# Where the additions of z run, where fourteen early gelus stand, five more warm-up matmuls and another order of banks in a linear-attention and GEGLU kernel

## The chip, the cores and the metric

The kernel runs on one core of a Trainium2 chip. A core has a matmul engine (TensorE, PE in the profile; its weight loads are shown as PEld), three engines for elementwise work (VectorE or DVE, ScalarE or ACT, GpSimd or POOL), and SyncE (SP), which here issues nearly all DMAs. Matmuls write PSUM, a memory of eight banks; everything else lives in SBUF, and inputs and output lie in HBM. The metric is the device time of one execution in microseconds (us); lower is better.

## The reference

One input x of 2048 tokens by 576 channels is normalised (xn) and goes through two branches, whose outputs are added to x. Branch A is linear attention with 32 heads of 18 channels. Branch B is a GEGLU feed-forward network with 4608 hidden channels.

```python
xn = layernorm(x)
# A: linear attention
q, k, v = split_heads(xn @ wqkv)                       # 32 heads of 18 channels
phi = lambda t: where(t > 0, t + 1, exp(t)) + 1e-6
pq, pk = phi(q), phi(k)
kv  = einsum("bhsd,bhse->bhde", pk, v)
z   = einsum("bhsd->bhd", pk)                          # sum of phi(k) over all tokens
o   = (pq @ kv) / (pq . z + 1e-6)
# B: feed-forward
ffn = (gelu(xn @ w_gate) * (xn @ w_up)) @ w_down
out = x + merge_heads(o) @ wo + ffn
```

The change deals with z, the sum of phi(k) over the 2048 tokens, and with the first hidden units of branch B.

## The kernel before

Tokens lie in 16 tiles of 128 (n = 0 to 15). The 4608 hidden channels are 36 units of 128, and the feed-forward part runs in four rounds of 512 tokens.

**First stage.** A tile of x is loaded, normalised on VectorE or ScalarE, and transposed into xnT: tiles 0 to 3 with TensorE (L337), the others with DMA transposes (L345). Then TensorE computes K for all 16 tiles and Q for the first four, and between them the gate and up projections of the first 14 hidden units (RAW = 14) for the first 512 tokens, whose raw results are copied out as they are (`_Raw`, copy L444). The list `line` gives PE's order: k0, q0, k1, q1, k2, k3, g0 to g3, K4, g4, K5, g5 and so on to K13, g13, K14, K15, Q2, Q3. A small letter is a token computed with whole 128-row matmuls (L408); a capital K or Q and every g is done in two parts, p1 and p2 (L245), in which two 64-row halves of the array write two banks and then swap. An empty instruction on GpSimd (the "turn", L256) stands between the two parts. The p1 of a unit comes one unit ahead of the p2 of the unit before it.

After p2 of a K, ScalarE computes exp (L420), VectorE clamps it (L423, "clamp") and adds the positive part of K from PSUM (L429, "phi"); the result is pk. Only then is the unit's pair of banks free. Five early tokens (RAW_T: k0, q0, k1, q1, k3) are first copied raw (L415), and their exp, clamp and phi are done later, from about 40 us on. Each unit takes two banks from a ring of eight (`banks`, L119), so a K takes over the pair of the K two tokens earlier, and a g that of the g two units earlier. The head tokens (k0 to k3, q0, q1) use a ring of their own over banks 4, 5, 6, 7, 2, 3; the transposes use banks 0 and 1, and the warm-up matmuls (`spin`, L226: 35 products of a zero tile) bank 7.

The order of this stage is made by a small planner: every piece of work is a `step` with an engine, a length, a rank and what it comes after. `in_order` (L66) plays the steps through with these lengths and emits, on each engine, the able step of the lowest rank number next; a step with a high number is emitted only where nothing else can run. On the chip each engine then runs its own list strictly in this order.

**Additions of z.** pk of tiles 4 to 13 are added into z_sum on GpSimd (L548, nine instructions, the first of which adds tiles 4 and 5), each held back until the turn of K two tokens later; pk of tiles 0 to 3 are added into z_dve on VectorE (L550); tiles 14 and 15 follow in the Gram stage, where z_sum and z_dve are added into z_bf (L632). In all this is nine instructions on GpSimd and six on VectorE.

**Gram.** G = xnᵀ pk is computed in five products (`gram` L563, `gram_last` L571), each over all 16 token tiles into two banks, and copied to g_sb, one half by ScalarE and the other by VectorE (`gram_copy`, L579). Then `kv_part` multiplies G with the V weights, `z_stage` sums z_bf over the partitions with a matmul by ones, and `mask_pair` keeps the heads' own blocks. Between these, `gelu_now` (L558) finishes the 14 raw units: gelu of the raw gate on ScalarE (L560), times the raw up on VectorE (L561). Eleven of them stand between the products, three behind the mask. The four bank pairs of Gram come up again in the feed-forward part after the ring has been stepped three pairs further (L651).

**Feed-forward.** `gu_pair` (L730) does two hidden units: p1, p1, p2, p2, then per unit the gelu (L753) and the product with up (L754). After 36 units `_DownTile` (L829) multiplies with w_down and adds the attention part and x. The weights of the last twelve w_down rows (wd_c) are loaded over the memory of the raw up results.

Of the kernel before, what the change touches and what calls it, by code (L numbers as in the profile page):

```python
# [9 lines left out]
ALU = mybir.AluOpType  # L10
# [4 lines left out]
P = 128  # L15
# [70 lines left out]
def kernel(  # L86
# [29 lines left out]

    SYNC = mybir.DependencyInfo(mybir.DependencyClass.Sync, mybir.DependencyReason.DATA)
    LO, HI = slice(0, HP), slice(HP, P)
    banks, head_banks = _Ring(list(range(8))), _Ring([4, 5, 6, 7, 2, 3])  # L119

    def two_banks(ring=banks):
        return [ring.next(), ring.next()]
# [28 lines left out]
    xn = apool.tile([P, NS, XW], BF16, name="xn")  # L151
    g_sb = apool.tile([P, KT, D], BF16, name="g_sb")
    z_sum = apool.tile([P, D], F32, name="z_sum")
    z_dve = apool.tile([P, D], F32, name="z_dve")
    z_bf = apool.tile([P, D], BF16, name="z_bf")

    def load_x(n0, cnt, on=nc.sync):
# [130 lines left out]
    def step(name, engine, took, rank, after, call, ready=0.0, tail=0.0):  # L288
        steps[name] = _Step(engine, took, rank, after, call, ready, tail)
# [68 lines left out]
        load(("x", n), 0.58, 295, 7.0 + 2.5 * (n - 10), [], lambda n=n: load_x(n, 2), ready=6.0)  # L358

    for n in range(NS):  # L360
        first = 1.5 * n if n < 4 else 11.0 + 3.0 * (n - 4)
        both = n // 2 * 2
        after_x = [("x", both)] if n >= 4 else []
        x_at = X_AT[n] if n < 4 else 0.0
        if n < 4:
            step(("twin", n), "POOL", 0.2, first, [], lambda n=n: x_twin(n, 1), ready=x_at)
        elif n == both:
            step(("twin", n), "POOL", 0.25, first, after_x, lambda n=n: x_twin(n, 2))
        twin = ("twin", n if n < 4 else both)
        for h in range(2):  # L370
            step(("stats", n, h), "DVE", 0.42, first, after_x, lambda n=n, h=h: ln_half(n, h), ready=x_at)
        step(("aggr", n), "DVE", 0.16, first, [("stats", n, 0), ("stats", n, 1)], lambda n=n: ln_aggr(n), tail=0.05)
        if n < 6:
            step(("rstd", n), "ACT", 0.46, first, [("aggr", n)], lambda n=n: ln_rstd(n, 1))
        elif n == both:
            step(("rstd", n), "ACT", 0.46, first, [("aggr", n), ("aggr", n + 1)], lambda n=n: ln_rstd(n, 2))
        ready = [("rstd", n if n < 6 else both), twin]
        if NORM[n] == "A":
            step(("bias", n), "POOL", 0.27, first, ready[:1], lambda n=n: ln_bias(n))
            ready.append(("bias", n))  # L380
        on, took = ("ACT", 0.92) if NORM[n] == "A" else ("DVE", 0.45)
        if n < HEAD:
            for i, (k0, k1) in enumerate(((0, TP_CUT), (TP_CUT, KT))):
                c0, c1 = k0 * P, k1 * P
                step(("norm", n, i), on, took * (c1 - c0) / XW + 0.05, first, ready, lambda n=n, c0=c0, c1=c1: ln_norm(n, c0, c1), tail=0.05)
                step(("tp", n, i), "PE", 0.06 * (k1 - k0), 0, [("norm", n, i)] + ([("xnT", n - 1, i)] if n else []), lambda n=n, i=i: transposes(n, i), tail=0.15)
                eng = "DVE" if i else "ACT"
                step(("xnT", n, i), eng, 0.26 if i else 0.48, first, [("tp", n, i)], lambda n=n, i=i: tp_copy(n, i), tail=0.02)
            steps[("xnT", n)] = _Step("none", 0.0, first, [("xnT", n, 0), ("xnT", n, 1)], lambda: None, 0.0, 0.0)
        else:  # L390
            step(("norm", n), on, took, first, ready, lambda n=n: ln_norm(n), tail=0.05)
            load(("xnT", n), 1.25, 80, first + 2, [("norm", n)], lambda n=n: dma_transposes(n))
# [97 lines left out]
    for name in line:  # L490
        kind, n = name[0], int(name[1:])
        if kind == "t":
            for i in range(2):
                pe(("tp", n, i), 0, [], None)
            continue
        u = _Chain()
        u.name, u.at = name, clock
        if kind in "kq":
            t = _Token(kind.upper(), n, head_banks)
            for h in range(2):  # L500
                free = owner.get(tuple(t.banks), [])
                pe((kind, n, h), 0.6125, [("xnT", n)] + free, lambda t=t, h=h: t.whole(h), ready=W_AT[kind.upper()])
                if kind == "k" and h == 0 and n + 1 < HEAD:
                    for i in range(2):
                        pe(("tp", n + 1, i), 0, [], None)
            later = name in RAW_T
            if later:
                step(("raw", name), "ACT", 0.72, clock, [(kind, n, 1)], t.raw)
            ready, rank = (LATER, 60.0) if later else (0.0, clock)
            step(("exp", name), "ACT", 0.72, rank, [("raw", name) if later else (kind, n, 1)], t.exp, ready=ready)  # L510
            step(("clamp", name), "DVE", 0.25, rank, [("exp", name)], t.clamp)
            step(("phi", name), "DVE", 0.76, rank, [("clamp", name)], t.phi, tail=0.05)
            owner[tuple(t.banks)] = [("raw" if later else "phi", name)]
            clock += 1.35
            continue
        if kind in "KQ":
            u.body = _Token(kind, n)
            b = u.body.banks
            after = [("xnT", n), ("w", "twin")]
            t1, u.t2 = 0.615, 0.49  # L520
            u.p1 = u.body.unit.rows
            u.swap = u.body.unit.swap
            u.unit_p2 = u.body.unit.p2
            at = 0.0
        else:
            u.body = _Raw(n)
            b = u.body.two
            blk = n // GUB
            after = [("xnT", m) for m in range(TPC)] + ([("gu", blk, i) for i in range(2)] if blk else [])
            t1, u.t2 = 1.08, 0.865  # L530
            u.p1 = u.body.rows
            u.swap = lambda body=u.body: body.unit.swap()
            u.unit_p2 = lambda body=u.body: body.unit.p2()
            at = 0.0 if blk else 9.1
        after += owner.get(tuple(b), [])
        pe(("p1", name), t1, after, u.p1, ready=at)
        step(("turn", name), "POOL", 0.06, clock, [("p1", name)], u.swap, tail=0.05)
        clock += t1 + u.t2
        pending.append(u)
        if len(pending) == 2:  # L540
            p2_step(pending.pop(0))
    while pending:
        p2_step(pending.pop(0))

    def z_add(on, dst, n, first):
        on.tensor_tensor(out=dst[:], in0=pk[:, n - 1, :] if first else dst[:], in1=pk[:, n, :], op=ALU.add)

    for n in range(HEAD + 1, NS - 2):  # L548
        step(("z", n), "POOL", 1.30, 6.0, [("turn", f"K{n + 2}"), ("phi", f"K{n}")], lambda n=n: z_add(nc.gpsimd, z_sum, n, n == HEAD + 1))
    for n in range(1, HEAD):  # L550
        step(("z", n), "DVE", 0.80, 52.0, [("phi", f"k{n - 1}"), ("phi", f"k{n}")] + ([("z", n - 1)] if n > 1 else []), lambda n=n: z_add(nc.vector, z_dve, n, n == 1))

    for name in in_order(steps):
        steps[name].call()
# [69 lines left out]
    on_banks = [two_banks() for _ in range(4)]  # L624
    gelus = list(range(RAW))
    gram(0, on_banks[0])
    gelu_now(gelus.pop(0))
    for n in range(NS - 2, NS):
        z_add(nc.vector, z_dve, n, False)
    gram_copy(0, on_banks[0])  # L630
    gram(1, on_banks[1])
    nc.vector.tensor_tensor(out=z_bf[:], in0=z_sum[:], in1=z_dve[:], op=ALU.add)  # L632
    for _ in range(2):
        gelu_now(gelus.pop(0))
    gram_copy(1, on_banks[1])
    gram(2, on_banks[2])
    for _ in range(4):
        gelu_now(gelus.pop(0))
    gram_copy(2, on_banks[2])
    gram_last(on_banks[3])  # L640
    gelu_now(gelus.pop(0))
    gram_copy(4, on_banks[3])
    gram(3, on_banks[0])
    for _ in range(3):
        gelu_now(gelus.pop(0))
    gram_copy(3, on_banks[0])
    b4, b1 = on_banks[1]
# [3 lines left out]
    for _ in range(3):  # L651
        two_banks()
    mask_pair(kvT, b4, b1)
    for f in gelus:
        gelu_now(f)

    asmall_cm.__exit__(None, None, None)
    awork_cm.__exit__(None, None, None)
# [71 lines left out]
    def gu_pair(sc, k):  # L730
        blk = sc * NB + k
        units = []
        aside = m_last_unit() if blk == M_UNIT else None
        if aside:
            aside.p1()
        for i in range(GUB):
            b = two_banks()
            u = gu_unit(blk, i, b, nc.gpsimd)
            if blk > RAW // GUB:
                load_gu(blk + NWBUF - 1, i)  # L740
            u.p1()
            units.append((b, u))
        if sc == 0 and k == RAW // GUB:
            load_wo()
        elif wd_left:
            load_wd(*wd_left.pop(0))
        if aside:
            aside.p2()
            m_last_copy(aside)
        for i, (b, u) in enumerate(units):  # L750
            u.p2()
            gl = fwork.tile([P, SC], F32, name="gl")
            nc.scalar.activation(out=gl[:], in_=ps_all[:, b[0], :], func=ACT.Gelu_apprx_tanh)  # L753
            nc.vector.tensor_tensor(out=hT[:, GUB * k + i, :], in0=ps_all[:, b[1], :], in1=gl[:], op=ALU.mult)  # L754
            if den_jobs and ((i == 1 and 0 < k < NB - 1) if sc else 8 < k < 17):
                job, n = den_jobs.pop(0)
                job(n)
# [186 lines left out]
```

## Time and profile before

The median of three runs is 515.73 us (515.57 to 515.77).

| what | value |
|---|---|
| profiled execution, its own time | 515.68 us |
| its span, first to last instruction | 513.9 us |
| PE busy | 505.3 us, 98% |
| VectorE busy | 229.9 us, 45% |
| ScalarE busy | 152.9 us, 30% |
| GpSimd busy | 20.7 us, 4% |
| first K matmul (L408) | at 6.66 us |
| K4, the first K done in two parts | at 24.57 us |
| Gram begins (L566) | at 64.40 us |
| first unit of the feed-forward loop (L245 behind L593) | at 84.00 us |

How to read it: a group's line gives source line, engine, operation, what is written and read, shapes, then how often, busy time, the mean of one in nanoseconds, and the idle time of the engine just before, with what ended it. A line of the order of time begins with start and length in us; "idle before" stands in brackets with its releaser. A line of the waits gives who waited for whom, the total in us, how many times, and the longest. Busy times of engines overlap, so they do not add up to the span. Matmuls overlap in the array and their ends are modelled, so the distance from start to start tells their rate better than the length of one.

### The profile page before, as it was taken

The page shows a single profiled execution, that of the slowest core. Times are in us where ns is not written, and L with a number is a line of the kernel's source. Part 1 is how long each engine was busy: PE and PEld are TensorE (multiplying, and loading weights), DVE is VectorE, ACT ScalarE, POOL GpSimd, SP SyncE. Part 2 cuts the span into 40 slices and gives each one's busy share as a digit, 9 for nine tenths or more (in the row PEclk, how much of TensorE's full clock was granted, in tenths as well). Part 3 has the DMA queues.
Part 4 walks back from the last instruction along what each step waited for, and adds up shares of the span by engine and source line. Part 5 has one row for each costly group of instructions (what it writes and reads, how often), then busy time and mean ns, then how long its engine had stood idle before and what let it go on. Part 6 is the DMA issues. An engine that isn't in the chain of part 4 may idle for free.

```text
span 513.9 us, 11032 instructions
## 1 busy us (share of the span) xinstructions
PE 505.3 (98%) x4686; PEld 309.2 (60%) x4686; DVE 229.9 (45%) x473; ACT 152.9 (30%) x265; POOL 20.7 (4%) x41
## 2 busy tenths in 40 slices
PE   8999899999999999999999999999999999999997
PEld 6587576444877544444777544445777544445774
DVE  6937886567000665555000765554101655544101
ACT  4878454333200432233000523323000533222000
POOL 2114400000000000000000000000000000000000
PEclk9999999999999999999999999999999999999999
DMA  9989902996210345665000356564000465740000
GB/s 262 258 172 237 282 2 66 280 255 165 63 63 1 117 144 163 177 163 147 13 11 1 116 164 173 152 168 136 13 13 4 134 174 147 163 131 14 13 13 23
DMA packets 113610, 61.56 MB, mean 120 GB/s; under 512 B 23250, under 2 KB 113562, under 8 KB 113562
## 3 DMA queue, kind: packets, MB, share of 16 engines
q1 hardware_dynamic: 113418, 60.72, 45.1%
q8 instruction: 36, 0.59, 0.5%
q10 hardware_dynamic: 144, 0.15, 0.1%
q14 instruction: 12, 0.10, 0.1%
HBM read 53.75 MB, written 2.36 MB: 109 GB/s over the span
## 4 chain that ended last, share of the span: by engine, by line
PE 93%; DVE 4%; DMA 1%; issue 0%; POOL 0%; ACT 0%; SPq 0%; DVEq 0%; POOLq 0%
PE ps_all L245 57%; PE ps_all L859 28%; PE ps_all L566 3%; PE ps_all L864 3%; PE ps_all L408 1%; DVE hT L429 1%; DVE stats L296 1%; DVE phi_e L423 1%; DMA wqkv_sb<-in_A_wqkv_dram 1%; DMA x_sb<-in_A_x_dram 1%; PE ps_all L847 0%; PE ps_all L574 0%; PE ps_all L337 0%; PE ps_all L593 0%; DVE pq L429 0%
## 5 line engine op out<-in xcount | busy, mean ns | idle before, releaser
L245 PE MATMUL ps_all<-xnT,wg 64*128 64x512 bf16 x1152 | 273.5, 376 | 0.0
L245 PE MATMUL ps_all<-xnT,wu 64*128 64x512 bf16 x1152 | 273.4, 376 | 0.0
L245 PEld LDWEIGHTS <-wg 64*128 64x128 bf16 x1152 | 108.3, 94 | 65.2
L245 PEld LDWEIGHTS <-wu 64*128 64x128 bf16 x1152 | 108.3, 94 | 64.5
L754 DVE TENSOR_TENSOR hT<-ps_all,gl 128x512 bf16<-128x512 f32 x130 | 89.9, 692 | 105.7 <-ACT gl L753 105.6
L859 PEld LDWEIGHTS <-hT 128*128 128x128 bf16 x1152 | 110.9, 98 | 30.9 <-issue 1.3
L753 ACT ACTIVATE gl<-ps_all 128x512 f32<-128x512 f32 x130 | 77.6, 597 | 165.4 <-PE ps_all L245 165.0
L873 DVE TENSOR_TENSOR res<-ps_all,x_sb 128x288 bf16<-128x288 f32 (+2 forms) x32 | 13.8, 455 | 146.3 <-PE ps_all L864 88.1
L859 PE MATMUL ps_all<-wd_a,hT 128*128 128x288 bf16 (+2 forms) x512 | 68.3, 286 | 0.0
L245 PE MATMUL ps_all<-xnT,wr 64*128 64x512 bf16 x288 | 55.3, 376 | 0.0
L859 PE MATMUL ps_all<-hT 128*128 128x288 bf16 (+2 forms) x384 | 52.4, 286 | 0.0
L773 ACT ACTIVATE gl<-ps_all 128x288 f32<-128x288 f32 x24 | 9.2, 410 | 121.4 <-PE ps_all L245 118.5
L859 PE MATMUL ps_all<-wd_m,hT 128*128 128x288 bf16 (+2 forms) x256 | 36.7, 286 | 0.0
L245 PEld LDWEIGHTS <-xnT 64*128 64x128 bf16 x468 | 25.5, 94 | 10.4 <-issue 4.2
L245 PEld LDWEIGHTS <-wr 64*128 64x128 bf16 x288 | 14.6, 94 | 16.2 <-issue 0.2
L245 PE MATMUL ps_all<-wqkv_sb,xnT 64*128 64x288 bf16 x252 | 19.2, 283 | 3.6 <-DVE hT L429 2.8
L864 PE MATMUL ps_all<-m_sb,pqT 128*128 128x288 bf16 (+2 forms) x128 | 20.9, 286 | 0.0
L423 DVE TENSOR_SCALAR phi_e<-phi_e 128x576 bf16<-128x576 bf16 x20 | 12.4, 629 | 11.6 <-ACT phi_e L420 11.5
L566 PE MATMUL ps_all<-hT,xn 128*128 128x288 bf16 x128 | 16.0, 286 | 0.0
L444 ACT CAST hT<-ps_all 128x1024 bf16<-128x1024 f32 x14 | 14.1, 1008 | 5.8 <-PE ps_all L245 5.8
L566 PEld LDWEIGHTS <-xn 128*128 128x128 bf16 x128 | 12.4, 98 | 3.5 <-issue 0.5
L864 PEld LDWEIGHTS <-pqT 128*128 128x128 bf16 x128 | 12.4, 98 | 3.3
(82 smaller groups left out, 257.1 us busy)
## 6 DMA issues: line engine op xcount, KB each, us to landing
wg<-in_B_w_gate_dram SPq DMA_DIRECT2D x72, 256.0 KB, 3.0
wu<-in_B_w_up_dram SPq DMA_DIRECT2D x72, 256.0 KB, 3.7
wr<-in_B_w_gate_dram SPq DMA_DIRECT2D x36, 64.0 KB, 3.2
wr<-in_B_w_up_dram SPq DMA_DIRECT2D x36, 64.0 KB, 2.8
wd_a<-in_B_w_down_dram SPq DMA_DIRECT2D x4, 576.0 KB, 8.1
out_dram<-res SPq DMA_DIRECT2D x15, 144.0 KB, 1.8
wqkv_sb<-in_A_wqkv_dram SPq DMA_DIRECT2D x3, 576.0 KB, 4.8
x_sb<-in_A_x_dram SPq DMA_DIRECT2D x6, 288.0 KB, 5.6
```

The source lines that it names most:

```text
L245: return nc.tensor.matmul(self.outs[i], lhsT=self.lhs(i, rows, kt), rhs=self.rhs(i, rows, kt), start=start, stop=stop, skip_group_check=True,)
L296: nc.vector.bn_stats(out=ln_raw[n][:, h, :], in_=x_sb[:, n, h * HALF:(h + 1) * HALF])
L408: nc.tensor.matmul(self.unit.outs[i], lhsT=xnT[:, kt, self.n * P:(self.n + 1) * P], rhs=wqkv_sb[:, kt, c:c + HALF], start=(kt == 0), stop= ...
L423: nc.vector.tensor_scalar(out=self.e[:], in0=self.e[:], scalar1=1.0, scalar2=EPS_ATT if self.kind == "K" else 0.0, op0=ALU.min, op1=ALU.add,)
L444: nc.scalar.copy(out=hT[:, self.f:self.f + NF + 1:NF, :], in_=ps_all[:, self.two[0]:self.two[0] + 2, :],)
L566: nc.tensor.matmul(ps_all[:, two[hf], :HALF], lhsT=xn[:, n, kt * P:(kt + 1) * P], rhs=pk[:, n, hf * HALF:(hf + 1) * HALF], start=(n == 0), ...
L753: nc.scalar.activation(out=gl[:], in_=ps_all[:, b[0], :], func=ACT.Gelu_apprx_tanh)
L754: nc.vector.tensor_tensor(out=hT[:, GUB * k + i, :], in0=ps_all[:, b[1], :], in1=gl[:], op=ALU.mult)
L773: nc.scalar.activation(out=e[:, :HALF], in_=acc, func=ACT.Exp)
L859: nc.tensor.matmul(self.acc(hf), lhsT=hT[:, f, j * P:(j + 1) * P], rhs=wd(f)[:, self.parts[hf]], start=(f == 0 and not paired), stop=False ...
L864: nc.tensor.matmul(self.acc(hf), lhsT=pqT[:, c, self.ts], rhs=m_sb[:, c, self.parts[hf]], start=False, stop=(paired and c == 3), skip_grou ...
L873: nc.vector.tensor_tensor(out=self.res[:, hs], in0=self.acc(hf), in1=x_sb[:, self.n, hs], op=ALU.add)
```

## The change

Five edits:

- All fifteen additions of z go to VectorE as steps of rank 80, the last in line. They follow the order of `z_order`, in one chain through z_sum; the last writes z_bf. The tile z_dve and the three instructions in Gram go.
- The 14 gelus of the raw units: eight stay between the products of Gram (2, 3, 1 and 2 of them), none ahead of the first Gram copy and none behind the mask. The other six follow the first three units of the feed-forward loop, two behind each.
- Behind the transposes of tile 0 in PE's order stand five more warm-up matmuls, ahead of k0.
- The ring of banks runs 0, 1, 4, 5, 6, 7, 2, 3 instead of 0 to 7. The pairs stay the same; g1, g2 and g3 take other ones than before.
- The planner's rank for the tiles from 4 on starts at 9.0 instead of 11.0. In the order that results, ScalarE does the norm of tile 5 ahead of the raw copy of k3, and one small copy on GpSimd comes earlier.

The order of the DMAs on SP is the same, and so is PE's but for the five matmuls. VectorE's order in the first stage becomes: phi of K5, an addition, phi of K6, an addition, phi of K7, an addition, phi of K8, an addition, phi of K9, k0, an addition, k1, K10, k3, q0, K11, q1, an addition, K12, two additions, K13, two additions, K14, an addition, K15, Q2, Q3, four additions.

```diff
-    banks, head_banks = _Ring(list(range(8))), _Ring([4, 5, 6, 7, 2, 3])
+    banks, head_banks = _Ring([0, 1, 4, 5, 6, 7, 2, 3]), _Ring([4, 5, 6, 7, 2, 3])
...
-        first = 1.5 * n if n < 4 else 11.0 + 3.0 * (n - 4)
+        first = 1.5 * n if n < 4 else 9.0 + 3.0 * (n - 4)
...
                 pe(("tp", n, i), 0, [], None)
+            pe("spin", 0.27, [], lambda: spin(5))
             continue
...
-    def z_add(on, dst, n, first):
-        on.tensor_tensor(out=dst[:], in0=pk[:, n - 1, :] if first else dst[:], in1=pk[:, n, :], op=ALU.add)
-
-    for n in range(HEAD + 1, NS - 2):
-        step(("z", n), "POOL", 1.30, 6.0, [("turn", f"K{n + 2}"), ("phi", f"K{n}")], lambda n=n: z_add(nc.gpsimd, z_sum, n, n == HEAD + 1))
-    for n in range(1, HEAD):
-        step(("z", n), "DVE", 0.80, 52.0, [("phi", f"k{n - 1}"), ("phi", f"k{n}")] + ([("z", n - 1)] if n > 1 else []), lambda n=n: z_add(nc.vector, z_dve, n, n == 1))
+    def z_add(i):
+        nc.vector.tensor_tensor(
+            out=(z_bf if i == NS - 1 else z_sum)[:], in0=pk[:, z_order[0], :] if i == 1 else z_sum[:], in1=pk[:, z_order[i], :],
+            op=ALU.add,
+        )
+
+    z_order = [4, 5, 6, 7, 8, 9, 10, 2, 11, 0, 12, 1, 13, 3, 14, 15]
+    for i in range(1, NS):
+        of = [("phi", f"{'k' if n < HEAD else 'K'}{n}") for n in z_order[i - (i == 1):i + 1]]
+        step(("z", i), "DVE", 0.76, 80.0, of + ([("z", i - 1)] if i > 1 else []), lambda i=i: z_add(i))
...
     gram(0, on_banks[0])
-    gelu_now(gelus.pop(0))
-    for n in range(NS - 2, NS):
-        z_add(nc.vector, z_dve, n, False)
     gram_copy(0, on_banks[0])
     gram(1, on_banks[1])
-    nc.vector.tensor_tensor(out=z_bf[:], in0=z_sum[:], in1=z_dve[:], op=ALU.add)
     for _ in range(2):
         gelu_now(gelus.pop(0))
     gram_copy(1, on_banks[1])
     gram(2, on_banks[2])
-    for _ in range(4):
+    for _ in range(3):
         gelu_now(gelus.pop(0))
...
     gram(3, on_banks[0])
-    for _ in range(3):
+    for _ in range(2):
         gelu_now(gelus.pop(0))
...
     mask_pair(kvT, b4, b1)
-    for f in gelus:
-        gelu_now(f)
...
             nc.vector.tensor_tensor(out=hT[:, GUB * k + i, :], in0=ps_all[:, b[1], :], in1=gl[:], op=ALU.mult)
+            for _ in range(min(len(gelus), 2)):
+                gelu_now(gelus.pop(0))
```

More of the change, by code (lines that the diff above doesn't have):

```diff
@@ L153 @@
     z_sum = apool.tile([P, D], F32, name="z_sum")
-    z_dve = apool.tile([P, D], F32, name="z_dve")
     z_bf = apool.tile([P, D], BF16, name="z_bf")
```

## The prediction

> **What bounds the kernel now.** I read the table of busy time and the chain first, then the waits of PE, then a table by stage, then the order of time around each wait.
>
> ```profile
> PE 505.3 (98%) x4686; PEld 309.2 (60%) x4686; DVE 229.9 (45%) x473; ACT 152.9 (30%) x265; POOL 20.7 (4%) x41
> PE 93%; DVE 4%; DMA 1%; issue 0%; POOL 0%; ACT 0%; SPq 0%; DVEq 0%; POOLq 0%
> ```
>
> TensorE is the bound nearly everywhere, so only what PE waits for can be won, and only 8.6 us of the span are not PE time. The waits of PE name it:
>
> ```profile
> PE ps_all L245 <- DVE hT L429: 2.8, 5, 0.8
> PE ps_all L229 <- DVE x_sb L193: 1.1, 1, 1.1
> PE ps_all L245 <- DMA xnT<-xn: 0.8, 1, 0.8
> PE ps_all L337 <- DVE xn L317: 0.6, 1, 0.6
> PE ps_all L408 <- ACT xnT L342: 0.4, 1, 0.4
> ```
>
> The reader is to see that the largest wait is for phi (L429, VectorE): the p1 of a K token waits until phi has emptied the bank pair it takes over, that of K two tokens earlier. The table by stage (stretch, length, then busy time of PE, PEld, DVE, ACT, POOL) says where VectorE is full:
>
> ```profile
> 24.00:43.00 19.00, 18.34 (x215) 16.14 (x217) 8.35 (x19) 15.78 (x24) 5.16 (x8) 1.00 0.94 178
> 43.00:64.40 21.40, 18.65 (x231) 12.61 (x225) 19.11 (x27) 12.88 (x18) 9.31 (x7) 1.00 1.03 272
> 64.40:84.00 19.60, 19.60 (x190) 15.84 (x189) 14.05 (x25) 11.20 (x22) 0.00 (x0) 1.00 0.00 1
> 84.00:107.00 23.00, 23.00 (x218) 10.54 (x218) 14.67 (x28) 7.09 (x14) 0.57 (x1) 1.00 0.93 234
> ```
>
> From 43 to 64.4 us VectorE works 89% of the time, POOL adds z beside it, and PE loses time; in Gram (64.4 to 84) PE loses none. The order of time shows why VectorE is full:
>
> ```profile
> 24.57 1.16 PE L245 MATMUL ps_all<-wqkv_sb,xnT 64*128 64x288 bf16 x10 [0.77 <-DMA xnT<-xn]
> ...
> 41.20 1.28 POOL L546 TENSOR_TENSOR z_sum<-z_sum,hT 128x576 f32<-128x576 f32 x1 [1.27 <-PE ps_all L245]
> 41.22 1.42 DVE L423 TENSOR_SCALAR phi_e<-phi_e 128x576 bf16<-128x576 bf16 x1 [2.04 <-ACT phi_e L420]
> 42.75 0.76 DVE L429 SCALAR_TENSOR_TENSOR hT<-ps_all,phi_e 128x576 bf16<-128x576 f32 x1
> 43.56 0.79 PE L245 MATMUL ps_all<-wqkv_sb,xnT 64*128 64x288 bf16 x10 [0.18 <-DVE hT L429]
> 44.10 0.31 DVE L423 TENSOR_SCALAR phi_e<-phi_e 128x576 bf16<-128x576 bf16 x1 [0.59 <-ACT phi_e L420]
> ...
> 55.30 1.72 POOL L546 TENSOR_TENSOR z_sum<-z_sum,hT 128x576 f32<-128x576 f32 x1 [2.55 <-DVE hT L429]
> 55.80 1.38 DVE L423 TENSOR_SCALAR phi_e<-phi_e 128x576 bf16<-128x576 bf16 x1
> 57.29 0.76 DVE L429 SCALAR_TENSOR_TENSOR hT<-ps_all,phi_e 128x576 bf16<-128x576 f32 x1
> 58.10 0.79 PE L245 MATMUL ps_all<-wqkv_sb,xnT 64*128 64x288 bf16 x10 [0.62 <-DVE hT L429]
> ```
>
> The clamp (L423) takes 0.31 us alone and 1.38 to 1.42 us while POOL adds z; it ends when the addition ends, then come phi and the waiting PE.
>
> **The change, part by part.**
>
> *Additions of z.* POOL loses nine, 1.28 to 1.72 us each. VectorE goes from six (three between the phis, two and the sum in Gram) to fifteen: four before 43 us, seven between the phis of K9 to K15, four behind Q3's phi. One takes 0.76 us, about 0.78 from start to start. What goes: the mean clamp of all 20 is 0.629 us against 0.31 alone, so 20 x 0.32 = 6.4 us of contention, of which 1.1 is the clamp at 41.22 and some 5 us lie in the full stage. What comes there is four more additions, 3.0 us. So 19.1 - 5 + 3 = 17 us in a stage which, without PE's waits, is 21.4 - 3.8 = 17.6 us long: tight, so places matter more than sums.
>
> What the waits are worth: the profile's idle before the five p1 is 0.18 + 0.37 + 0.84 + 0.62 + 0.74 = 2.75 us, counted from modelled ends of 0.283 us matmuls whose successors start after 0.06 us when nothing holds them (44 in 2.87 us at 61.60). 2.75 + 5 x 0.22 = 3.85; I take 3.8 us.
>
> Do they go? The loop gives PE one K and one g unit each 3.05 us (K p1 at 30.94, 33.98, 37.03 us). Counted from the start T of a K's p1, its p2 ends at T + 3.05, exp (0.65) at T + 3.9, and phi must be done at T + 6.1. Clamp and phi take 1.02 us from start to start, so VectorE may begin up to T + 5.0, and between one K's phi and the next clamp lie 2.0 us for other work. From the order of VectorE's instructions in the changed kernel: before K10 stand phi of k0, an addition and phi of k1 (1.02 + 0.78 + 1.02 = 2.8 us, 0.8 over the 2.0, slack then 0.3); before K11 k3 and q0 (2.04, slack 0.3); before K12 q1 and one addition (1.8, slack 0.6); before K13 and K14 two additions each (1.5). No K waits by this count, the least slack is 0.3 us. Hops that I read as 0.1 us may be 0.2, so I leave a remainder of 0.3 us. Bounds: nothing left (-3.8) and, if each of the seven additions pushes its K by all of 0.76 us, 5.3 us left (+1.5).
>
> Behind Q3 three additions and the one that writes z_bf hold VectorE for 3.1 us and delay its half of the first Gram copy by about 2 us. Its banks come up again in gram(3), some 10 us later (three stretches of 32 matmuls, 3.9 + 3.9 + 2.1 us), and z_bf is read in z_stage at the end of Gram: 0.
>
> *Gelus.* Eleven stood in Gram and three behind the mask; now eight in Gram and six behind the first three units of the FFN, two each. Such a unit costs VectorE 0.69 + 2 x 0.63 = 1.95 us and ACT 0.60 + 2 x 0.56 = 1.7, against 18 matmul pairs of 0.108 = 1.94 us on PE. A unit's banks come back four units (7.8 us) later, and its result leaves them within 5 us of its p1: 0, covered by that ring; without it, six times 0.63 us, 3.8. The down tiles (L859) read hT first at 127.3 us, and wd_c overwrites the raw halves only from the fourth pair of the FFN on: 0. The DMA order on SP is unchanged, instruction by instruction.
>
> *Spare matmuls.* Five of 0.107 us fill 0.53 us between the last transpose (5.99 us) and the first K matmul at 6.66, where PE waits for the ACT copy. K matmuls start every 240 ns up to 10.28 us and every 122 ns after it, although the granted clock is 1.00 in every stretch shown. Bounds: 0.5 us later at the first K, or one slow stretch of 3.4 us gone (up to 1.7 us earlier). Either way PE then stands at K4, which waits till 24.95 us for a landing that no part of the change touches:
>
> ```profile
> 21.10 0.02 SPq L166
> 21.12 0.03 issue
> 21.15 3.76 DMA wqkv_sb<-in_A_wqkv_dram
> 24.91 0.04 issue
> 24.95 12.96 PE ps_all L245 x153
> ```
>
> PE is ready there from 23.63 us on, 1.3 us early, and the DMA queue's earlier issues wait for earlier landings, not for an engine. I take 0; if this landing did come earlier with PE, 1.3 us more could go.
>
> The Trainium skill, "TensorE: Matmul & The Clock Gate", Part 1, says that the array's clock is released by a free-running window of about 3.4 us of activity. By it the spare matmuls could release the window that begins near 6.9 us, and the sum would be 1.7 us lower if PE did not wait at K4; the wait at 24.57 us speaks against counting it.
>
> *Banks and rank.* g1, g2, g3 take pairs freed at 14.78 (raw copy of q1), 17.45 (phi of k2) and about 18.6 us (raw copy of k3, which now stands behind the norm of tile 5, 0.9 us); their p1 start at 17.8 us or later, g3's past 20: 0.
>
> Sum: -3.8 + 0.3 = -3.5 us. The profiled execution took 515.68 us (span 513.9), 0.05 under the median of 515.73, so **512.2 us**.
>
> **Rivals.**
>
> A, VectorE stays the limit: its first-in first-out queue holds a K's clamp behind an addition or a raw token and one to three of the 3.8 us stay. For it: 17 of 17.6 us, slacks of 0.3. Against it: the 2.0 us between two K tokens cover all but one slot. Time 513.8 us (about 1.9 left).
>
> B, slower: the same queue, but an addition ahead of every K from K10 to Q2 pushes phi past T + 6.1. The price is up to 7 x 0.76 = 5.3 us, that is 517.2 us; it decides when more than 3.8 us are left, 0.54 us for each of the seven. Against it: only the slot before K10 exceeds 2.0 us.
>
> C, no change: the long clamps are not POOL's doing, or waits of the same size come up at another place (the fourth unit of the FFN, K4 with a later landing). Then 515.7 us. Against it: the pairs of rows above, and clamps of 0.31 us whenever POOL is still.
>
> D, the landing at 24.91 us moves forward as well: 512.2 - 1.3 = 510.9 us.
>
> **How the numbers follow.** Chances: forecast 0.60 (own range 511.9 to 512.9, that is 0 to 1.0 us left), A 0.23, B 0.09, C 0.05, D 0.03. The range reaches from just under the forecast, 511.6, over most of A to 514.3; B, C, D and the edge of A stay out, about 2 in 10. A measurement of this kernel can tell 0.2%, 1.03 us: faster than 514.7 hold the forecast, A and D, 0.86; C 0.05; B 0.09.
>
> **What would show it.** Right: all clamps near 0.31 us, no z_sum on POOL, PE's idle before K10 to Q2 under 0.3 us each, Gram beginning near 60.9 us instead of 64.4, PE without gaps from there on. The first K matmuls may become faster early, with a longer wait before K4 and the same 24.9 us at its end. Wrong: a wait of PE for L429 of more than 1 us in total, a clamp that starts late behind L546, a gap of PE in units 4 to 8 of the FFN, or K4 past 25.5 us.

## The result and the profile after

The changed kernel takes 512.37 us (median of four runs, 512.34 to 512.48) against 515.74 us: a ratio of 0.9936, with a 95% interval of 0.9919 to 0.9953. The forecast was 512.2 us. The profiled execution took 512.38 us, its span 510.7 us, 3.2 us less than before. Of the executions below, one of the run with the additions alone (530.34 us, the one that was profiled) and one of the last run (1374.85 us) were far slower than the others of their kernels, and medians and ratios leave these two out. Source lines in this profile are one lower than before up to the planner's loop; phi is L428, the clamp L422, p1 and p2 are L244.

The table of busy time and the chain:

```profile
PE 503.3 (99%) x4691; PEld 311.6 (61%) x4691; DVE 229.6 (45%) x482; ACT 152.4 (30%) x265; POOL 8.0 (2%) x32
PE 96%; DMA 1%; issue 1%; DVE 0%; ACT 0%; POOL 0%; POOLq 0%
```

VectorE has dropped out of the chain (4% before), although its busy time is the same to 0.3 us: the time that the longer clamps took is about what the added additions take. The waits of PE:

```profile
PE ps_all L244 <- DMA xnT<-xn: 1.4, 1, 1.4
PE ps_all L228 <- DVE x_sb L192: 1.1, 1, 1.1
PE ps_all L244 <- POOLq L255: 1.0, 1, 1.0
PE ps_all L336 <- DVE xn L316: 0.6, 1, 0.6
PE ps_all L407 <- ACT xnT L341: 0.2, 1, 0.2
```

The five waits for phi are gone. Two other lines have grown or are new: the wait before K4 is 1.4 instead of 0.8 us, and there is one of 1.0 us for GpSimd's queue. The table by stage shows that from 43 us to the beginning of Gram, at 61.13 us (64.40 before), PE has no idle time, and none in the two stages after it:

```profile
24.00:43.00 19.00, 17.97 (x209) 15.85 (x211) 9.76 (x21) 15.23 (x24) 1.23 (x5) 1.00 0.85 177
43.00:60.90 17.90, 17.90 (x234) 16.14 (x230) 16.10 (x30) 12.84 (x19) 0.52 (x1) 1.00 1.10 283
60.90:80.50 19.60, 19.60 (x190) 15.68 (x186) 13.36 (x24) 8.56 (x16) 0.06 (x1) 1.00 0.18 48
80.50:103.50 23.00, 23.00 (x220) 10.59 (x220) 16.43 (x31) 9.58 (x18) 0.57 (x1) 1.00 0.91 229
```

The groups of the clamp before (L423) and after (L422), from the groups by line of each kernel:

```profile
L423 DVE TENSOR_SCALAR phi_e<-phi_e 128x576 bf16<-128x576 bf16 x20 | 12.4, 629 | 11.6 <-ACT phi_e L420 11.5
```

```profile
L422 DVE TENSOR_SCALAR phi_e<-phi_e 128x576 bf16<-128x576 bf16 x20 | 6.1, 305 | 9.4 <-ACT phi_e L419 9.4
```

6.3 us of VectorE time have gone from the same twenty instructions. The tightest part of the new order, round K10 and K11:

```profile
48.25 0.30 DVE L422 TENSOR_SCALAR phi_e<-phi_e 128x576 bf16<-128x576 bf16 x1
48.66 0.76 DVE L428 SCALAR_TENSOR_TENSOR hT<-ps_all,phi_e 128x576 bf16<-128x576 f32 x1
49.09 1.37 PE L244 MATMUL ps_all<-wqkv_sb,xnT 64*128 64x288 bf16 x18
...
51.76 0.76 DVE L428 SCALAR_TENSOR_TENSOR hT<-ps_all,phi_e 128x576 bf16<-128x576 f32 x1
52.13 1.37 PE L244 MATMUL ps_all<-wqkv_sb,xnT 64*128 64x288 bf16 x18
```

A PE group here is 8 matmuls of p2 and 10 of the next p1, which begins 0.49 us after the group (49.58 us for K12, 52.62 for K13). Phi of K10 ends at 49.42 and phi of K11 at 52.52 us: 0.16 and 0.10 us to spare.

The K4 landing, from the chain in order of time:

```profile
18.53 0.03 POOLq L255
18.56 0.05 issue
18.60 2.89 PE ps_all L244 x25
21.50 3.78 DMA wqkv_sb<-in_A_wqkv_dram
25.28 0.04 issue
25.32 35.88 PE ps_all L244 x439
```

K4 waits for two landings. Its first matmul needs the transpose of tile 4 and starts at 24.93 us (24.57 before); this is the wait that the list names. The second one also needs the weights in the chain above: it starts at 25.32 us, 0.37 us later than before (24.95). From there to Gram PE needs 35.88 us in one piece where it took 39.5.

SyncE's list of DMA issues shows by which way the landing came later. First before, then after:

```profile
16.75 1.82 SPq L184 DMA_DIRECT2D wu<-in_B_w_up_dram  x1
19.00 2.04 SPq L345 DMA_TRANSPOSE xnT<-xn  x1
21.15 1.17 SPq L166 DMA_DIRECT2D wqkv_sb<-in_A_wqkv_dram  x2
```

```profile
18.52 0.44 SPq L183 DMA_DIRECT2D wu<-in_B_w_up_dram  x1
19.48 1.91 SPq L344 DMA_TRANSPOSE xnT<-xn  x1
21.50 1.16 SPq L165 DMA_DIRECT2D wqkv_sb<-in_A_wqkv_dram  x2
```

The load of up weights (wu) is issued 0.01 to 0.02 us after x of tiles 10 and 11 has landed (16.74 us before, 18.50 now). The transpose of tile 4 is issued 0.08 us after x of tiles 12 and 13 has landed (18.92 before, 19.40 now), and the weights for K4 stand behind it.

### The profile page after: what moved, and what is told of

It is laid out like the page before. It is cut to its first block, busy times and chain, and to the rows that moved or that the text cites. A ratio compares the mean times of both kernels' runs of the same rounds, so it can differ in the third digit from the quotient of the medians.

```text
span 510.7 us, 11034 instructions
## 1 busy us (share of the span) xinstructions
PE 503.3 (99%) x4691; PEld 311.6 (61%) x4691; DVE 229.6 (45%) x482; ACT 152.4 (30%) x265; POOL 8.0 (2%) x32
## 4 chain that ended last, share of the span: by engine, by line
PE 96%; DMA 1%; issue 1%; DVE 0%; ACT 0%; POOL 0%; POOLq 0%
PE ps_all L244 60%; PE ps_all L858 28%; PE ps_all L569 3%; PE ps_all L863 3%; PE ps_all L407 1%; DMA wqkv_sb<-in_A_wqkv_dram 1%; DMA x_sb<-in_A_x_dram 1%; PE ps_all L846 0%; PE ps_all L577 0%; PE ps_all L336 0%; PE ps_all L596 0%; DVE stats L295 0%; PE ps_all L798 0%; DVE xn L316 0%; ACT phi_e L419 0%
## 5 line engine op out<-in xcount | busy, mean ns | idle before, releaser
L244 PE MATMUL ps_all<-xnT,wu 64*128 64x512 bf16 x1152 | 273.5, 376 | 1.0 <-POOLq L255 1.0
L244 PE MATMUL ps_all<-xnT,wg 64*128 64x512 bf16 x1152 | 273.5, 376 | 0.0
L244 PEld LDWEIGHTS <-wu 64*128 64x128 bf16 x1152 | 108.2, 94 | 65.0 <-POOLq L255 1.5
L244 PEld LDWEIGHTS <-wg 64*128 64x128 bf16 x1152 | 108.2, 94 | 64.0
L244 PE MATMUL ps_all<-xnT,wr 64*128 64x512 bf16 x288 | 55.6, 376 | 0.0
L244 PEld LDWEIGHTS <-xnT 64*128 64x128 bf16 x468 | 26.5, 94 | 6.4 <-DMA xnT<-xn 1.9
L244 PEld LDWEIGHTS <-wr 64*128 64x128 bf16 x288 | 14.9, 94 | 15.9 <-issue 0.2
L244 PE MATMUL ps_all<-wqkv_sb,xnT 64*128 64x288 bf16 x252 | 18.8, 283 | 1.5 <-DMA xnT<-xn 1.4
L244 PE MATMUL ps_all<-wo,xnT 64*128 64x288 bf16 x216 | 13.7, 283 | 0.0
```

Of the source, the lines that this page charges most:

```text
L244: return nc.tensor.matmul(self.outs[i], lhsT=self.lhs(i, rows, kt), rhs=self.rhs(i, rows, kt), start=start, stop=stop, skip_group_check=True,)
```

## The experiments

The theory: the additions on GpSimd stretch the clamps on VectorE, phi comes late, and PE waits for its banks; all other parts of the change are hidden. The rivals: the early clock or the moved gelus carry part of the gain; VectorE is near its limit and only the exact place of the additions keeps PE from waiting.

All times are medians of repeated runs; the kernel before took 515.9 to 516.0 us in the same sessions.

### The additions alone

```diff
 (the kernel before, with the new z_add, z_order and steps of rank 80; z_dve and the three
  instructions in Gram go; nothing else is changed)
```

> The kernel before, with the additions of z moved to VectorE in the new order and nothing else of the change. Theory (the additions on GpSimd stretch the clamps, phi comes late, PE waits for its banks): the whole gain is here, 512.2 to 512.7 us, all clamps about 0.31 us, no wait of PE for L429 after 25 us, first K matmuls still 240 ns apart. Rival (the gain needs the early clock or the moved gelus): 514 us or more, with Gram beginning after 62.5 us.

Measured: 512.46 us, ratio 0.9932 [0.9918, 0.9946], that of the whole change (0.9936). The gain is in this part. One expectation failed: the first five K matmuls take 0.80 us in its profile, without any spare matmuls, and are not 240 ns apart.

### All other parts, without the additions

```diff
 (the changed kernel with the old z_add on GpSimd and VectorE, z_dve, and the three instructions in Gram)
```

> The changed kernel with the additions of z put back as they were (nine on GpSimd, six on VectorE): spare matmuls, order of banks, rank and gelus stay changed. Theory: 515.3 to 516.2 us, clamps of 1.4 us beside GpSimd's additions, about 3.8 us of waits before K10 to Q2. The first K matmuls may be 122 ns apart from the start, and the wait before K4 longer by what that gains. Rival (early clock or gelus carry part of the gain): below 514.7 us.

Measured: 515.91 us, ratio 1.000 [0.9991, 1.0009]. The waits of PE:

```profile
PE ps_all L245 <- DVE hT L429: 2.8, 5, 0.8
PE ps_all L245 <- DMA xnT<-xn: 1.4, 1, 1.4
...
PE ps_all L245 <- POOLq L256: 0.9, 1, 0.9
```

The waits for phi are back, to the tenth of a microsecond, and the two early waits are those of the changed kernel. So these two belong to the early part. The other parts are worth nothing in sum.

### GpSimd's additions left out

```diff
-    for n in range(HEAD + 1, NS - 2):
-        step(("z", n), "POOL", 1.30, 6.0, [("turn", f"K{n + 2}"), ("phi", f"K{n}")], ...)
...
-    nc.vector.tensor_tensor(out=z_bf[:], in0=z_sum[:], in1=z_dve[:], op=ALU.add)
+    nc.vector.tensor_tensor(out=z_bf[:], in0=z_dve[:], in1=z_dve[:], op=ALU.add)
```

> The kernel before without GpSimd's nine additions, so the sum of k over tiles 4 to 13 is left out and VectorE adds nothing more than before. Theory: contention alone made the waits, so 511.8 to 512.5 us, and at most 0.3 us under the run with all additions on VectorE: these cost nothing there. Rival (VectorE is full also without contention, its order of raw tokens makes part of the waits): 513 us or more, with waits of PE for L429 of over 1 us.

Measured: 512.04 us, ratio 0.9928 [0.9916, 0.9941], and PE has no wait for phi:

```profile
PE ps_all L228 <- DVE x_sb L192: 1.1, 1, 1.1
PE ps_all L244 <- DMA xnT<-xn: 1.0, 1, 1.0
PE ps_all L336 <- DVE xn L316: 0.6, 1, 0.6
PE ps_all L407 <- ACT xnT L341: 0.4, 1, 0.4
```

With nothing else changed, the end of GpSimd's work brings the whole gain. The nine additions that VectorE takes over cost PE nothing that the profiles show: from K4's landing to Gram it needs 35.81 us here (24.97 to 60.78 us) and 35.81 us in the changed kernel (25.32 to 61.13). The 0.3 us by which this run lies under the changed kernel is the earlier landing, 24.93 instead of 25.28 us.

### Useless additions on GpSimd in the changed kernel

```diff
+    z_spare = apool.tile([P, D], F32, name="z_spare")
+    for n in range(HEAD + 1, NS - 2):
+        step(("y", n), "POOL", 1.30, 6.0, [("turn", f"K{n + 2}"), ("phi", f"K{n}")], lambda n=n: nc.gpsimd.tensor_tensor(
+            out=z_spare[:], in0=pk[:, n - 1, :] if n == HEAD + 1 else z_spare[:], in1=pk[:, n, :], op=ALU.add))
```

> The changed kernel with nine additions of the old shape and places on GpSimd, whose sum nobody reads. Theory: clamps beside them take 1.4 us again, VectorE has some 20.5 us of work in the stage where PE has 17.9, so PE waits more than before: 516 to 518 us. Rival (the waits came from the chain of z itself or from its place, not from GpSimd working beside VectorE): 512.4 us, within 0.5.

Measured: 517.42 us, ratio 1.0028 [1.0018, 1.0039], slower than before. The stage from 43 to 64.4 us, and the order of time in it:

```profile
43.00:64.40 21.40, 18.05 (x221) 12.20 (x218) 20.50 (x29) 13.20 (x18) 8.71 (x6) 1.00 1.08 282
```

```profile
48.02 1.28 POOL L558 TENSOR_TENSOR z_spare<-z_spare,hT 128x576 f32<-128x576 f32 x1 [1.77 <-DVE z_sum L546]
48.13 1.78 DVE L428 SCALAR_TENSOR_TENSOR hT<-hT,phi_e 128x576 bf16<-128x576 bf16 x1
...
56.15 1.72 POOL L558 TENSOR_TENSOR z_spare<-z_spare,hT 128x576 f32<-128x576 f32 x1 [2.79 <-PE ps_all L244]
56.66 1.38 DVE L422 TENSOR_SCALAR phi_e<-phi_e 128x576 bf16<-128x576 bf16 x1
```

VectorE is busy for 20.50 of 21.40 us, and PE waits 3.4 us in five places for phi and 0.8 more before Gram. An addition whose result nobody reads brings the loss back, so it is neither the chain of z nor a semaphore: it is the two engines working at once. One thing was not expected: not only the clamp but also the phi of a raw token, whose two inputs both lie in SBUF, is stretched, from 0.76 to 1.78 us.

### Without the spare matmuls

```diff
-            pe("spin", 0.27, [], lambda: spin(5))
```

> The changed kernel without the five spare matmuls. Theory (K4 waits for its DMA whatever PE did before): within 0.4 us of the changed kernel, 512.0 to 512.7 us; K matmuls 240 ns apart up to some 10 us, the wait before K4 shorter by 0.4 to 1 us, its end within 0.4 us of 25.3. Rival (the early clock carries part of the gain): 513.2 us or more.

Measured: 512.12 us, ratio 0.9925 [0.9912, 0.9937]: the time as expected, the clock not. The first K matmuls of this run without spare matmuls:

```profile
6.41 0.79 PE L407 MATMUL ps_all<-wqkv_sb,xnT 128*128 128x288 bf16 x5 [0.37 <-ACT xnT L341]
```

Five take 0.79 us as in the changed kernel (at 6.63 us), not the 1.38 us of the kernel before. So the spare matmuls are not needed for that.

### The gelus put back

```diff
     gram(0, on_banks[0])
+    gelu_now(gelus.pop(0))
...
-    for _ in range(3):          # behind gram(2)
+    for _ in range(4):
...
-    for _ in range(2):          # behind gram(3)
+    for _ in range(3):
...
     mask_pair(kvT, b4, b1)
+    for f in gelus:
+        gelu_now(f)
+    gelus = []
```

> The changed kernel with the gelus where they stood: eleven in Gram, one of them ahead of its first copy, three behind the mask. Theory (hidden in either place): 512.0 to 512.7 us, no gap of PE from Gram on in either. Rival (their new place wins or costs): 0.5 us or more away from 512.4.

Measured: 512.19 us, ratio 0.9928 [0.9916, 0.9941]. PE is busy for the whole of the stretches 60.9 to 80.5 and 80.5 to 103.5 us in this run as in the changed kernel. Their place is free of cost either way.

### The additions at a high rank

```diff
-        step(("z", i), "DVE", 0.76, 80.0, ...
+        step(("z", i), "DVE", 0.76, 6.0, ...
```

> The changed kernel with the additions of z at rank 6 in the planner instead of 80, so that each stands as soon as its phi is there and the late raw tokens stand behind them. Theory (between two K tokens VectorE has some 2.0 us for other work, and a phi that starts up to a microsecond late delays nobody): 512.0 to 512.8 us, no wait of PE for L428 after 25 us in sum over 0.4 us. Rival (VectorE is at its limit, and only the lowest rank keeps the additions out of the way): 513.5 us or more, with PE waiting for L428 before K10 to Q2.

Measured: 513.23 us, ratio 0.9946 [0.9933, 0.996], between the two forecasts. No K waits; one wait is new:

```profile
PE ps_all L569 <- DVE hT L428: 0.8, 1, 0.8
```

It stands at the first matmul of Gram, at 62.00 us, whose banks are those of K14: two additions and a raw phi stand in front of the phi of K14, in the part without g units where a pair of banks comes round faster. But the additions are not all of this wait:

```profile
60.34 0.58 POOL L622 MEMSET g_sb<- 128x576 bf16 x1 [21.03 <-PE ps_all L244]
60.34 0.74 DVE L422 TENSOR_SCALAR phi_e<-phi_e 128x576 bf16<-128x576 bf16 x1
61.18 0.76 DVE L428 SCALAR_TENSOR_TENSOR hT<-ps_all,phi_e 128x576 bf16<-128x576 f32 x1
```

K14's clamp begins together with the clearing of g_sb on GpSimd and takes 0.74 us instead of 0.30; in the changed kernel the clearing (60.38 us) falls beside an addition on VectorE, which keeps its 0.75 us. So by estimate (0.74 less 0.30) 0.44 of the 0.8 us is again GpSimd beside VectorE, and the rank alone is worth the rest, at the end of the stage and not at K10 to Q2.

### More work ahead of K4

```diff
-    line = [..., "g2", "g3"]
+    line = [..., "g2", "g3", "g4"]
     for i in range(12):
-        line += [f"K{i + 4}"] + ([f"g{i + 4}"] if i + 4 < RAW else [])
+        line += [f"K{i + 4}"] + ([f"g{i + 5}"] if i + 5 < RAW else [])
```

> The changed kernel with unit g4 ahead of K4 in PE's order, so that PE has 1.95 us of work while K4's DMA is on its way; each later g stands one K earlier. Theory (the wait before K4 is what is left to win in this stage, 1.6 to 1.8 us of PE standing still): 510.5 to 511.2 us, the wait before K4 under 0.4 us. Rival (g4's own weights land too late, or K14 to Q3, now without a g between K13 and K14, wait for phi): 512 us or more, with the wait moved there.

Measured: 510.56 us, ratio 0.9894 [0.988, 0.9907]. The wait before K4 is gone (K4 starts at 25.09 us), and 1.8 us with it, about what PE had stood still there.

The same without the spare matmuls:

```diff
-            pe("spin", 0.27, [], lambda: spin(5))
```

> The same with g4 ahead of K4, but without the five spare matmuls. Theory (the early clock was hidden by the wait before K4, and with g4 there the wait no longer covers it): 0.7 to 1.7 us over the run with g4 ahead and spare matmuls, 511.3 to 512.5 us. Rival (the clock's start does not depend on these five matmuls, or PE still waits): within 0.4 us of it.

Measured: 510.41 us, ratio 0.9892 [0.9877, 0.9907], no different. The profile shows why this could not tell anything apart: its first K matmuls take 0.79 us too. What the early clock is worth once K4 no longer waits was therefore not measured.

### Two units ahead of K4, and the turn of g0 freed

```diff
-    line = [..., "g3", "g4"]
+    line = [..., "g3", "g4", "g5"]
     for i in range(12):
-        line += [f"K{i + 4}"] + ([f"g{i + 5}"] if i + 5 < RAW else [])
+        line += [f"K{i + 4}"] + ([f"g{i + 6}"] if i + 6 < RAW else [])
...
+    steps[("twin", 10)].after = steps[("twin", 10)].after + [("turn", "g1")]
```

> The run with g4 ahead of K4, with g5 ahead of it as well and the copy of tiles 10 and 11 on GpSimd put behind the turns of g0 and g1. Theory (the turn of g0 waits on GpSimd behind that copy, whose DMA lands late, 0.9 to 1.3 us of PE; with it gone K4 needs more work ahead of its DMA, which g5 gives): no wait of PE for GpSimd's queue, none before K4, 509.3 to 510.0 us. Rival (six tokens in a row at the end, K12 to Q3, wait for phi, or g5's order of loads costs as much): 510.3 us or more.

Measured: 509.20 us, ratio 0.9874 [0.9859, 0.9889], the fastest. The two edits were not run apart. All waits of PE in the whole run:

```profile
PE ps_all L228 <- DVE x_sb L192: 1.1, 1, 1.1
PE ps_all L336 <- DVE xn L316: 0.5, 1, 0.5
```

Behind the first transposes, at 5.4 us, the list has no wait of PE any more.

## Why the prediction was right, and where it was off

**The additions.** Right in mechanism and nearly in size. The clamps came down to 0.305 us, 6.3 of the 6.4 us that the means gave. VectorE had 16.1 us of work in the shorter stage, 17 had been worked out. No K waits, as the count of free time between two K tokens said; but the slack it gave as 0.3 us measured 0.16 (K10) and 0.10 us (K11). The count was right by little.

**The price of the waits.** 3.8 us was 0.2 too much: from K4's landing to Gram PE took 39.5 us and takes 35.9, 3.6 less. The 0.3 us that was left as a remainder at the K tokens did not appear; 0.37 us came at K4 instead. That the sum came so near is luck in this: a term that did not come made up for one that had been put at zero.

**K4.** "PE then stands at K4, which waits till 24.95 us for a landing that no part of the change touches" held for the price, zero, as the two runs without and with only these parts show. But the landing came at 25.28 us, 0.37 later, and this made the -3.6 a -3.27 at the beginning of Gram. The prediction took the landing for one that the change does not touch, and said itself that the issues before it wait for earlier landings; one of these, that of x of tiles 12 and 13, came 0.48 us later, which was not looked for. Landings lie at 24.9 us in the two profiles where the matmul rate rose late (before, and the run without GpSimd's additions) and at 25.0 to 25.4 us in the others that have this wait.

**The spare matmuls.** Their price was right, the link to the early rate was not shown: 3.4 us of slow matmuls are gone in all seven profiles with the spare matmuls, but also in three of the five without them. They are not needed for it; whether they make it surer is open. The page "TensorE: Matmul & The Clock Gate", Part 1, of the Trainium skill calls the window free-running and the number of slow matmuls variable from run to run; the runs agree, as the rate rises between 4.6 and 6.4 us in ten profiles and at 9.9 to 10.3 us in two. The 1.7 us of the early rate never reached the end, as the waits at g0 and before K4 took them.

**Gelus, banks, Gram.** Nothing, as worked out. The VectorE half of the first Gram copy starts at 67.31 us, 2.2 after ScalarE's at 65.14 (2 had been said), and nobody waits for it.

**Rivals.** A (one to three us stay) and B (VectorE as a slower queue) fall for the order as it is; the run with a high rank shows B's mechanism at one place, Gram's first matmul, for about half of a wait of 0.8 us. C falls with the run without GpSimd's additions and the one with useless ones. D was wrong in its premise: PE's earlier arrival does not bring the landing forward, but work put ahead of K4 wins what D would have won, and more.

**What was missed.** A new wait: PE stands 1.0 us at the p2 of g0, since the turn of g0 stands on GpSimd behind the copy of tiles 10 and 11, which waits for its DMA. The queue of GpSimd had been looked at for the additions that leave it, not for the copy that stays. The wait before K4 covers it. This wait and the later landing before K4 come from the same place: x lands later, 1.76 us for tiles 10 and 11 and 0.48 us for tiles 12 and 13.

## What to carry to other kernels

An engine with 4% of busy time can be the one that costs: look for instructions of one form with two durations, and for what runs beside the long ones. Before work is moved to the engine that the chain names, count the free time between its urgent instructions, and not only its sum. A gain ahead of a fixed landing is worth nothing until there is work to put in front of the wait; the wait itself tells how much.

## What the runs showed that was not expected

- Beside an addition on GpSimd (fp32, 128x576, about 1.28 us at its shortest) VectorE's clamp takes 1.38 to 1.42 us instead of 0.31, and a phi with both inputs in SBUF 1.72 to 1.78 instead of 0.76, while a phi that reads PSUM keeps 0.76. The long clamps end about 0.16 us after GpSimd's addition, these phis about 0.6 us after it. The Trainium skill, "GPSIMD Engine Reference", section 8 (Key points), names contention for VectorE instructions in a 2-port mode or with two SBUF inputs; the runs agree for the two inputs, as the phi from SBUF is stretched and the one from PSUM is not; which mode the clamp runs in no run shows.
- The matmul rate changes once, from about 107 to 56 ns for 128 columns, between 4.6 and 6.4 us or at about 10 us, early in seven of seven profiles with the five spare matmuls and in three of five without; the granted clock in the rows before and after the rise stands at 1.00 in the profiles of the kernels before and after.
- In the ten profiles with the early rate x of tiles 10 and 11 lands at 18.2 to 18.5 us, in the two with the late one at 16.7 to 16.8. Why is open: the two were seen together, and no run parts them.
